# Two weight loads moved to ScalarE's queue in front of its table load, two scalar loads moved to SyncE

## The chip, the cores and the metric

The kernel runs on one core of a Trainium2 chip (trn2). The metric is the device time of one execution in microseconds (us), given as the median of several runs. The engines are TensorE (PE, matrix products), VectorE (DVE), ScalarE (ACT), GpSimd (POOL) and SyncE (SP, which here only issues transfers). Each runs its own instructions strictly in the order in which the program gives them. DMA transfers run on 16 DMA engines; SP's transfers are in one queue, those that ACT issues in another.

## The reference

Attention with a gated memory read, and behind it two feed-forward networks. B, H, S, D are 4, 8, 576, 64; there are 2304 tokens, the model width is 512 and the hidden width 2048.

```python
def _attn_ref(q, k, v, M_prev, z_prev, beta):
    scores = scale * np.matmul(q, k.transpose(0, 1, 3, 2))    
    local = np.matmul(a, v)
    q_p = phi(q)                                              
    mem_out = np.einsum('bhsd,bhde->bhse', q_p, M_prev) / mem_norm
    g = 1.0 / (1.0 + np.exp(-beta))[None, :, None, None]
    return g * mem_out + (1 - g) * local

def _moe_ref(x, w_in, w_out, s, b):
    r = np.maximum(x @ w_in, 0.0)
    return (s * (r * r) + b) @ w_out

def _moe2_ref(x, w_in, w_out):
    h = x @ w_in
    return (h * np.tanh(softplus(h))) @ w_out
```

The weights arrive as 64-bit floating-point numbers. [...]

## The kernel before

The work is cut into steps. Each step names an engine, an estimated duration, a due time (`prio`) and the buffers that it reads and writes. `Plan.order` (L234) is a list scheduler: it runs the steps in its own simulated time with these estimates, always starts the ready step that is due first on each engine, and the order in which it starts them is the order in which the instructions are written. Nothing is reordered on the chip. For a DMA step it reckons (L284 to L286) that transfers run one behind the other, the first no sooner than 0.35 us after its issue, and land 1.6 us and a `lag` after their turn. Where PE would have nothing to do between 7 and 165 us of the planned time, the plan puts in products of a block of zeros (`zero_product`, L1262).

The attention works in units, one for each batch entry and head. For the first batch entry each unit is cut in two; the first halves (row tiles 0 to 2) are due 2.36 us apart. Such a unit loads qz (the queries and z, L481), qk (transposed queries and keys, L476) and vm (L645) on SP's queue; POOL, ACT and DVE make phi and its norm (L500 to L506); PE makes the scores (L536); DVE adds the mask and takes the least value (L545); ACT makes exponentials (L554); POOL scales (L557, L571); PE transposes (L598) and multiplies by the values (L626); SP stores the result to `x_d` (L640).

Beside the units run the conversions of the first network's weights: 32 pieces, `convert` (L676), each 128 rows by 512 numbers, 512 KB. A piece is loaded to a raw buffer (L693, SP's queue), two ACT steps scale its high and low words (L700, L705), three DVE steps put them together (L707, L709, L711), ACT rounds the result to the high part (L717) and DVE makes the low part (L720). The first pieces are due 3.0 us apart, piece 0 at 0.0. Pieces 0 and 1 have their raw buffers in `stage`, at columns 0 and 1024; pieces 2 to 5 in weight tiles that are still unused. The first network begins as soon as its inputs are there: PE L803 and L877, with the scalars s and b (tile `sb`) read in L848 to L859. The second network (from L993) follows behind it.

Ahead of all steps stands a fixed beginning (L388 to L397): ACT issues the load of beta, loads its function table, and issues the loads of s and b, each of them one value spread over 128 partitions; DVE and ACT make the gates of beta and the block of zeros.

Of the kernel before, what the change touches and what calls it, by code (L numbers as in the profile page):

```python
# [9 lines left out]
F32 = mybir.dt.float32  # L10
F32R = mybir.dt.float32r
BF16 = mybir.dt.bfloat16
I32 = mybir.dt.int32
# [5 lines left out]
PSUM = bass.MemoryType.PSUM  # L19
DRAM = bass.MemoryType.DRAM  # L20

P = 128
MASKED = -1.0e30
HUGE = 3.0e38
PE, ACT, DVE, POOL, DMA = range(5)
# [41 lines left out]
def on(letter):  # L67
    return {"A": ACT, "D": DVE, "P": POOL}[letter]
# [111 lines left out]
class Plan:  # L180
# [29 lines left out]
    def add(self, engine, us, prio, f, r=(), w=(), after=(), keep=(), share=1.0):  # L210


        bufs = list({id(b): b for b in (*r, *w, *keep) if b.ring is not None}.values())
        new = [b for b in bufs if b.maker is None]
        waits = {id(s): s for b in r for s in b.writers}
        waits.update((id(s), s) for s in after)
        s = Step(engine, us, prio, f, list(waits.values()), bufs, new)
        s.share = share
        s.left = len(waits)
        for x in waits.values():  # L220
            x.next.append(s)
        for b in bufs:
            b.users += 1
            if b.maker is None:
                b.maker = s
            elif id(b.maker) not in waits:
                b.maker.next_start.append(s)
                s.left += 1
        for b in w:
            b.writers.append(s)  # L230
        self.steps.append(s)
        return s
# [100 lines left out]
def attention_then_two_ffn(ctx: ExitStack, tc: tile.TileContext, qk, qz, vm, beta,  # L333
# [3 lines left out]
    nc = tc.nc  # L337
# [22 lines left out]
    NONE = 5  # L360
    plan = Plan()
    add = plan.add
# [13 lines left out]
    sb = const.tile([P, 2], F32, name="sb")  # L376
# [8 lines left out]
    y_in = {j: Buf() for j in range(NT // N1)}  # L385
    wi_in, wo_in, wi_split = ({} for _ in range(3))

    nc.scalar.dma_start(igate[:, 1], beta.partition_broadcast(P))  # L388
    nc.scalar.preload_act_table_set("natural_log_exp_and_others")
    nc.scalar.dma_start(sb[:, 0:1], s1.partition_broadcast(P))  # L390
    nc.scalar.dma_start(sb[:, 1:2], b1.partition_broadcast(P))

    nc.vector.tensor_scalar(igate[:, 0], igate[:, 1], -1.0, 80.0, op0=ALU.mult, op1=ALU.min)
    nc.vector.tensor_scalar_min(igate[:, 1], igate[:, 1], 80.0)
# [1 line left out]
    nc.vector.tensor_scalar_add(igate, igate, 1.0)  # L396
    nc.scalar.copy(zeros, mask[:, :P])  # L397

    psum = ctx.enter_context(tc.tile_pool(name="psum", bufs=1, space=PSUM))
    banks = [Bank(psum.tile([P, 512], F32, name=f"bank{i}")) for i in range(8)]  # L400
    stage = Home(ctx.enter_context(tc.tile_pool(name="stage", bufs=1, side="right")), "stage", 3072)
    m1 = ctx.enter_context(tc.tile_pool(name="m1", bufs=1))
    small, att = ExitStack(), ExitStack()
    m1s = small.enter_context(tc.tile_pool(name="m1s", bufs=1))
# [256 lines left out]
    def weight_bufs():  # L661
        for nm in ("wih", "wil", "woh", "wol"):
            for r in range(NR):
                W[nm, r] = Buf(R[nm, r], [P, NCC, 512], F32R)

    def w_at(nm, r, j):
        return W[nm, r].t[:, j]

    def raw_buf(r, k):

        i = (8 * r + k) % 6
        if r > 1 or i < 2:
            return Buf(R["raw"], [P, 1024], I32)
        return Buf(R[("wih", "wil", "woh", "wol")[i - 2], 2], [P, 2048], I32)

    def convert(layer, prio, which, r, j, raw, after=()):  # L676


        w_in, w_out = ((w_in1, w_out1), (w_in2, w_out2))[layer - 1]
        fc = r * FPR + j  # L680
        src = w_in[j * P:(j + 1) * P, r * 512:(r + 1) * 512] if which == "in" else w_out[fc * P:(fc + 1) * P, :]
        w = Buf(R["w32"], [P, 512], I32)

        def words():
            return raw.t[:, :1024].rearrange("p (n two) -> p n two", two=2)

        def limbs():
            return raw.t[:, :1024].bitcast(U16).rearrange("p (n four) -> p n four", four=4)

        def f32():  # L690
            return w.t.bitcast(F32)

        add(DMA, 1.5, prio, lambda: nc.sync.dma_start(words(), src.bitcast(I32).rearrange("p (n two) -> p n two", two=2)),  # L693
            w=[raw], after=after).lag = 1.4 if layer == 1 else 3.0

        e = on((C_W if layer == 1 else C2_W)[j])
        add(e, 0.567 if e == ACT else 0.335, prio,
            (lambda: nc.scalar.activation(f32(), words()[:, :, 1].bitcast(F32), AF.Copy, scale=2.0 ** -112)) if e == ACT else  # L700
            (lambda: nc.vector.tensor_scalar(f32(), words()[:, :, 1].bitcast(F32), 2.0 ** -112, None, op0=ALU.mult)),
            [raw], [w])

        low_words = Buf()
        add(ACT, 0.567, prio, lambda: nc.scalar.activation(words()[:, :, 0], words()[:, :, 0].bitcast(U32), AF.Copy,  # L705
                                                          scale=2.0 ** -29), [raw], [low_words])
        add(DVE, 0.335, prio, lambda: nc.vector.tensor_scalar(w.t, w.t, 3, None, op0=ALU.logical_shift_left), [w], [w])  # L707
        signed = Buf()
        add(DVE, 0.542, prio, lambda: nc.vector.tensor_scalar(limbs()[:, :, 1], limbs()[:, :, 3], 0x8000, None, op0=ALU.bitwise_and),  # L709
            [raw, low_words], [signed])  # L710
        add(DVE, 0.605, prio, lambda: nc.vector.tensor_tensor(w.t, w.t, words()[:, :, 0], op=ALU.add), [raw, signed, w], [w])  # L711
        if layer == 1:
            hi, lo = f"w{which[0]}h", f"w{which[0]}l"
            hi_dve, lo_dve = C_HI[j] == "D", C_LO[j] == "D"
            half = Buf()
            add(DVE if hi_dve else ACT, 0.335 if hi_dve else 0.52, prio,
                lambda: (nc.vector.tensor_copy if hi_dve else nc.scalar.copy)(w_at(hi, r, j), f32()), [w],  # L717
                [W[hi, r], half])
            add(DVE if lo_dve else POOL, 0.6 if lo_dve else 1.23, prio,
                lambda: (nc.vector if lo_dve else nc.gpsimd).tensor_tensor(w_at(lo, r, j), f32(),  # L720
                                                                           w_at(hi, r, j).bitcast(F32), op=ALU.subtract),
                [w, half], [W[lo, r]])
        return w
# [426 lines left out]
        unit(0, h, PRE_A + STEP_A * h, (TA,), PLACE_A[h % 4])  # L1150
    for h in range(H):
        unit(0, h, PRE_B + STEP_B * h, (TB,), PLACE_B[h])
    raws = [raw_buf(i // 8, i % 8) for i in range(len(pieces))]
    weight_bufs()
    start = 0.0
    for i, p in enumerate(pieces):
        convert(1, start, *p, raws[i])
        start += CONV[i // 8]
# [15 lines left out]
    for i in range(len(seq) + LAG1):  # L1174
        if i < len(seq):
            j, fc = seq[i]
# [4 lines left out]
            n = len(plan.steps)  # L1181
# [4 lines left out]
        if i >= LAG1:  # L1186
            j, fc = seq[i - LAG1]
            n = len(plan.steps)
# [3 lines left out]
            if fc == NFC - 1:  # L1192
                n = len(plan.steps)
# [17 lines left out]
    n = len(plan.steps)  # L1211
# [3 lines left out]
    def converted_piece(which, r, j):  # L1215
        n = len(plan.steps)
        w = convert(2, CONV2, which, r, j, Buf(R["raw"], [P, 1024], I32), [opened])
        raw_steps.extend(plan.steps[n:])
        return w
# [17 lines left out]
    n = len(plan.steps)  # L1237
# [72 lines left out]
```

## Time and profile before

| | us |
|---|---|
| median of 3 runs | 1012.31 (1010.95 to 1012.92) |
| the profiled execution's own time | 1011.65 |
| its span, first to last instruction | 1009.7 |
| PE busy | 993.8 |
| DVE busy | 861.0 |
| ACT busy | 717.6 |
| POOL busy | 205.2 |

An engine is busy while an instruction of its own computes; issuing a DMA is not counted. Idle time of an engine counts only where another engine, or the end, waits for it. Matrix products are pipelined, so a busy PE is not PE at its peak.

### The profile page before, as it was taken

The numbers are of one execution on the slowest core, as the hardware profiler recorded it, in microseconds if no ns is written. First come the engines' busy times: TensorE is split into PE (matmuls) and PEld (weight loads), VectorE is DVE, ScalarE is ACT, GpSimd is POOL, SyncE is SP. The second block draws the span as 40 slices with busy tenths as digits, with TensorE's granted clock in tenths as the row PEclk, the third lists the DMA queues.
The fourth block names the chain that finished last, engine by engine and source line by source line (L and its number), as shares of the span: only waits on it lengthen the run. The fifth ranks groups of instructions, "written<-read, shape, count | busy, mean of one in ns | idle before, by whom it ended". The sixth has DMA issues, their size and how long they took to land.

```text
span 1009.7 us, 19024 instructions
## 1 busy us (share of the span) xinstructions
PE 993.8 (98%) x6274; PEld 904.4 (90%) x6274; DVE 861.0 (85%) x2232; ACT 717.6 (71%) x1606; POOL 205.2 (20%) x330
## 2 busy tenths in 40 slices
PE   7999999999999999999999999999999999999998
PEld 4758798999999999999888888899989998899987
DVE  6899999999999999986788886269996789967876
ACT  5988897888988889876778998446763466534552
POOL 5851123433443335320000000000110000100010
PEclk9999999999999999999999999999999999999999
DMA  9664563333533342215899986468787666766565
GB/s 270 182 201 128 158 199 99 112 92 101 144 90 91 97 123 85 85 54 182 264 279 299 298 280 225 155 229 276 231 287 253 210 225 204 262 222 216 166 224 172
DMA packets 88977, 188.54 MB, mean 187 GB/s; under 512 B 8752, under 2 KB 63024, under 8 KB 81584
## 3 DMA queue, kind: packets, MB, share of 16 engines
q1 hardware_dynamic: 81392, 135.95, 43.5%
q0 software_dynamic: 7056, 51.38, 15.0%
q8 instruction: 49, 0.80, 0.3%
q14 instruction: 48, 0.39, 0.1%
q10 hardware_dynamic: 432, 0.01, 0.0%
HBM read 144.32 MB, written 42.99 MB: 186 GB/s over the span
## 4 chain that ended last, share of the span: by engine, by line
PE 86%; DVE 5%; ACT 3%; issue 2%; DMA 2%; POOL 2%; SPq 0%; DVEq 0%; POOLq 0%; ACTq 0%
PE bank L877 19%; PE bank L803 19%; PE bank L1009 17%; PE bank L1081 10%; PE bank L626 6%; PE bank L1083 5%; PE bank L598 4%; PE bank L540 2%; PE bank L536 2%; PE bank L541 2%; POOL Pt L571 1%; PE bank L1078 1%; DMA woh<-wi_split_d 1%; DVE Pt L545 1%; ACT Pt L554 1%
## 5 line engine op out<-in xcount | busy, mean ns | idle before, releaser
L1009 PE MATMUL bank<-wi,woh 128*128 128x384 f32 x420 | 95.2, 335 | 0.1
L557 POOL TENSOR_SCALAR Pt<-ex,nm 128x64 f32<-128x64 f32 x148 | 70.8, 495 | 114.2 <-DVE nm L506 50.6
L1081 PE MATMUL bank<-wol,S 128*128 128x512 f32 x252 | 90.7, 391 | 0.0
L554 ACT ACTIVATE Pt<-Pt,mx 128x64 f32<-128x64 f32 (+4 forms) x148 | 81.7, 554 | 11.9 <-DVE mx L545 11.4
L1081 PE MATMUL bank<-woh,S 128*128 128x512 f32 x228 | 82.1, 392 | 0.0
L990 POOL DMA_DIRECT2D wol<-wo_split_d x16 | 8.7, 541 | 339.6 <-DVE wi L732 261.7
L1009 PE MATMUL bank<-wi,wol 128*128 128x384 f32 x300 | 76.0, 334 | 0.0
L1009 PEld LDWEIGHTS bank<-wi,woh 128*128 128x128 f32 x420 | 74.6, 188 | 1.4 <-DMA woh<-wi_split_d 0.6
L1083 PE MATMUL bank<-wol,S 128*128 128x256 f32 x252 | 70.6, 280 | 0.0
L598 PE MATMUL bank<-ident,Pt 128*128 128x128 f32 x432 | 65.7, 279 | 3.2 <-POOL Pt L571 3.1
L571 POOL TENSOR_SCALAR Pt<-Pt,rs 128x64 f32<-128x64 f32 (+2 forms) x68 | 53.9, 823 | 64.6 <-DVE rs L576 50.4
L606 DVE TENSOR_TENSOR PTl<-bank,PTh 128x128 fp32r<-128x128 f32 (+1 forms) x144 | 64.2, 481 | 1.3 <-ACT PTh L603 0.7
L1083 PE MATMUL bank<-woh,S 128*128 128x256 f32 x228 | 63.9, 280 | 0.0
L545 DVE CUSTOM_DVE_ANT_0 Pt<-bank,mask 128x320 f32<-128x320 f32 (+3 forms) x148 | 59.8, 417 | 4.4 <-PE bank L536 3.0
L598 PEld LDWEIGHTS bank<-ident,Pt 128*128 128x128 f32 x432 | 49.4, 142 | 9.5 <-POOL Pt L571 7.0
L603 ACT CAST PTh<-bank 128x128 fp32r<-128x128 f32 (+1 forms) x144 | 55.3, 431 | 2.7 <-PE bank L598 1.4
L1081 PEld LDWEIGHTS bank<-wol,S 128*128 128x128 f32 x252 | 47.2, 187 | 9.8
L1009 PEld LDWEIGHTS bank<-wi,wol 128*128 128x128 f32 x300 | 54.1, 188 | 0.3
L877 PE MATMUL bank<-gl,woh 128*128 128x256 f32 x320 | 53.8, 290 | 0.0
L877 PE MATMUL bank<-gh,wol 128*128 128x256 f32 x320 | 53.3, 289 | 0.0
L877 PE MATMUL bank<-gh,woh 128*128 128x256 f32 x320 | 52.1, 285 | 0.0
L803 PE MATMUL bank<-xh,wi 128*128 128x256 f32 x320 | 51.5, 288 | 0.6 <-DVE rt L854 0.4
(291 smaller groups left out, 3123.6 us busy)
## 6 DMA issues: line engine op xcount, KB each, us to landing
woh<-wo_split_d POOLq DMA_DIRECT2D x17, 1024.0 KB, 5.1
wol<-wo_split_d POOLq DMA_DIRECT2D x16, 1024.0 KB, 5.6
qk<-in_qk SPq DMA_DIRECT2D x24, 608.0 KB, 3.8
stage<-in_w_out SPq DMA_DIRECT2D x23, 512.0 KB, 4.3
wo_split_d<-high SPq DMA_DIRECT2D x44, 256.0 KB, 3.7
stage<-in_w_in SPq DMA_DIRECT2D x21, 512.0 KB, 5.0
wol<-wi_split_d POOLq DMA_DIRECT2D x10, 1024.0 KB, 6.0
stage<-wi_d SPq DMA_DIRECT2D x24, 384.0 KB, 3.7
```

The costliest lines, as they stand in the source:

```text
L545: nc.vector.tensor_tensor_reduce(Pt[t].t[:, D + lo:D + hi], ps.t[:, :hi - lo], mask[:, SP - w + lo:SP - w + hi], -SCALE, mx.t[:, t:t + 1] ...
L554: nc.scalar.activation(Pt[t].t[:, D:w + D], Pt[t].t[:, D:w + D], AF.Exp, bias=mx.t[:, t + i:t + i + 1], scale=-1.0, accum_out=rs.t[:, t:t ...
L557: add(POOL, 0.48, lambda: nc.gpsimd.tensor_scalar(Pt[t].t[:, :D], ex.t[:, t, :], nm.t[:, t:t + 1], 1.0, op0=ALU.mult, op1=ALU.mult), [ex, ...
L571: (nc.vector if e == DVE else nc.gpsimd).tensor_scalar(x, x, r, None, op0=ALU.mult)
L598: nc.tensor.transpose(ps.t[:, c - c0, :], Pt[t].t[:, c * P:(c + 1) * P], ident)
L606: nc.vector.tensor_tensor(PT[1].t[:, at_], ps.t[:, :n], PT[0].t[:, at_].bitcast(F32), op=ALU.subtract)
L626: nc.tensor.matmul(o.rearrange("p (t q) -> p t q", q=P), v, x.t[:, f[0]:f[-1] + 1:f[1] - f[0] if len(f) > 1 else 1, :], start=(c == 0 and ...
L803: nc.tensor.matmul(ph, w_at(nm, r, cc)[:, o:o + P], x_at(x, cc), start=(part == 0 and cc == 0), stop=(part == 2 and cc == NCC - 1))
L877: nc.tensor.matmul(acc[ec // per].t[:, (ec % per) * n:(ec % per + 1) * n], w_at(nm, r, jj)[:, ec * P:(ec + 1) * P], t(x), start=(big and f ...
L1009: nc.tensor.matmul(ps.t[:, :H2], w[i // 4].t[:, j, kk, i % 4], x[kk].t[:, k], start=begin and part == kk == 0, stop=part == 2 and kk == 1, ...
L1081: nc.tensor.matmul(acc[t].t.rearrange("p (k n) -> p k n", n=DH), s.t[:, 0, t * P:(t + 1) * P], x.t[:, :, q % 4], start=q == 0, stop=False, ...
L1083: nc.tensor.matmul(acc[t].t[:, :DH], s.t[:, 1, t * P:(t + 1) * P], x.t[:, 0, q % 4], start=False, stop=q == NQ2 - 1, skip_group_check=True)
```

## The change

The loads of weight pieces 0 and 1 leave the plan. They are issued by ACT, right behind the load of beta and in front of the function table's load, to the same places in `stage`. The pool of PSUM banks and `stage` are allocated earlier for that; no instruction belongs to it. In the plan each of the two loads becomes a step without an instruction on the plan's sixth engine (`NONE`), which says that the piece is there after 5.5 us and, behind it, after 1.0 us more. The loads of s and b leave ACT's queue and become two DMA steps of SP, due at 12.0.

```diff
     nc.scalar.dma_start(igate[:, 1], beta.partition_broadcast(P))
+    for j in range(2):
+        nc.scalar.dma_start(stage.tile([P, 1024], I32, 1024 * j, "raw").rearrange("p (n two) -> p n two", two=2),
+                            w_in1[j * P:(j + 1) * P, :512].bitcast(I32).rearrange("p (n two) -> p n two", two=2))
     nc.scalar.preload_act_table_set("natural_log_exp_and_others")
-    nc.scalar.dma_start(sb[:, 0:1], s1.partition_broadcast(P))
-    nc.scalar.dma_start(sb[:, 1:2], b1.partition_broadcast(P))
...
-        add(DMA, 1.5, prio, lambda: nc.sync.dma_start(words(), src.bitcast(I32).rearrange("p (n two) -> p n two", two=2)),
-            w=[raw], after=after).lag = 1.4 if layer == 1 else 3.0
+        if layer == 1 and which == "in" and r == 0 and j < 2:
+            add(NONE, (5.5, 1.0)[j], prio, lambda: None, w=[raw])
+        else:
+            add(DMA, 1.5, prio, lambda: nc.sync.dma_start(words(), src.bitcast(I32).rearrange("p (n two) -> p n two", two=2)),
+                w=[raw], after=after).lag = 1.4 if layer == 1 else 3.0
...
+    add(DMA, 0.2, 12.0, lambda: nc.sync.dma_start(sb[:, 0:1], s1.partition_broadcast(P)))
+    add(DMA, 0.2, 12.0, lambda: nc.sync.dma_start(sb[:, 1:2], b1.partition_broadcast(P)))
     raws = [raw_buf(i // 8, i % 8) for i in range(len(pieces))]
```

## Rows read from the trace of the kernel before

**Rows 1.** The page: busy us (share of the span) and instructions of each engine.

```profile
PE 993.8 (98%) x6274; PEld 904.4 (90%) x6274; DVE 861.0 (85%) x2232; ACT 717.6 (71%) x1606; POOL 205.2 (20%) x330
```

**Rows 2.** Busy time by stretch: from:to, length, engines, clock, DMA share, GB/s.

```profile
0.00:10.00 10.00, 4.02 (x11) 2.87 (x12) 3.19 (x13) 3.19 (x6) 3.15 (x11) 1.00 0.70 163
1.50:4.50 3.00, 0.00 (x0) 0.00 (x0) 0.57 (x2) 0.95 (x1) 1.08 (x4) 1.00 0.38 73
4.50:26.00 21.50, 18.75 (x57) 12.74 (x58) 16.04 (x60) 13.63 (x42) 13.14 (x19) 1.00 1.05 313
...
140.00:172.00 32.00, 30.59 (x240) 28.78 (x239) 31.77 (x87) 26.54 (x65) 10.11 (x13) 1.00 0.38 120
172.00:400.00 228.00, 227.22 (x1836) 223.34 (x1835) 221.07 (x712) 193.79 (x520) 89.84 (x144) 1.00 0.36 105
```

**Rows 3.** The same of the products of zeros alone (L1262): PE, PEld.

```profile
140.00:172.00 32.00, 6.26 (x36) 5.12 (x36) 1.00 0.38 120
```

**Rows 4.** The chain of waits, its beginning: start us, us, what.

```profile
2.54 5.63 DMA stage<-in_w_in
```

**Rows 5.** Timeline, 0 to 26 us: start, us, engine, line, operation [idle before <-releaser].

```profile
1.17 1.28 ACT L389 ACT_TABLE_LOAD   x1 [1.17 <-PEq L1297]
1.19 0.69 SPq L476 DMA_DIRECT2D wih<-in_qk  x1
1.20 0.43 ACTq L390 DMA_DIRECT2D sb<-in_s  x1
...
1.65 0.45 ACTq L391 DMA_DIRECT2D sb<-in_b  x1
...
2.54 0.43 SPq L693 DMA_DIRECT2D stage<-in_w_in  x1
...
4.55 0.22 ACT L395 ACTIVATE igate<-igate 128x16 f32<-128x16 f32 x1 [2.11 <-DVE igate L394]
...
6.50 0.23 DVE L498 TENSOR_SCALAR nm<-nm,igate 128x3 f32<-128x3 f32 x1
6.53 0.33 SPq L693 DMA_DIRECT2D stage<-in_w_in  x1
...
6.56 2.50 PE L536 MATMUL bank<-wih 64*128 64x64 f32 x6 [0.96 <-DMA wih<-in_qk]
...
8.19 0.66 ACT L700 ACTIVATE stage<-stage 128x512 f32<-128x512 f32 x1 [2.96 <-DMA stage<-in_w_in]
...
8.88 0.43 DVE L707 TENSOR_SCALAR stage<-stage 128x512 int32<-128x512 int32 x1 [2.15 <-ACT stage L700]
...
9.31 0.20 DVE L545 CUSTOM_DVE_ANT_0 Pt<-bank,mask 128x64 f32<-128x64 f32 x1
...
12.44 0.33 SPq L693 DMA_DIRECT2D woh<-in_w_out  x1
...
12.54 0.66 ACT L700 ACTIVATE stage<-stage 128x512 f32<-128x512 f32 x1
...
15.31 0.68 ACT L700 ACTIVATE stage<-wih 128x512 f32<-128x512 f32 x1 [1.31 <-DMA wih<-in_w_in]
...
25.89 0.70 ACT L700 ACTIVATE stage<-woh 128x512 f32<-128x512 f32 x1
```

**Rows 6.** DMA issues, each from a stretch around its issue: KB, us to landing.

```profile
wih<-in_qz SPq DMA_DIRECT2D x1, 128.0 KB, 3.0
wih<-in_qk SPq DMA_DIRECT2D x1, 192.0 KB, 5.3
stage<-in_w_in SPq DMA_DIRECT2D x1, 512.0 KB, 5.6
sb<-in_b ACTq DMA_DIRECT2D x1, 0.5 KB, 5.0
...
woh<-in_w_out SPq DMA_DIRECT2D x1, 512.0 KB, 7.3
```

**Rows 7.** The instructions that read `sb`, first of them: count, ns, first and last start.

```profile
L848 ACT ACTIVATE rt<-bank,sb x80: 448/474/511, 80.7 to 476.6; 128x256 f32<-128x256 f32 x80
```

More of the change, by code (lines that the diff above doesn't have):

```diff
@@ L386, in attention_then_two_ffn @@
     wi_in, wo_in, wi_split = ({} for _ in range(3))
+    psum = ctx.enter_context(tc.tile_pool(name="psum", bufs=1, space=PSUM))
+    banks = [Bank(psum.tile([P, 512], F32, name=f"bank{i}")) for i in range(8)]
+    stage = Home(ctx.enter_context(tc.tile_pool(name="stage", bufs=1, side="right")), "stage", 3072)
     nc.scalar.dma_start(igate[:, 1], beta.partition_broadcast(P))
+    for j in range(2):
+        nc.scalar.dma_start(stage.tile([P, 1024], I32, 1024 * j, "raw").rearrange("p (n two) -> p n two", two=2),
+                            w_in1[j * P:(j + 1) * P, :512].bitcast(I32).rearrange("p (n two) -> p n two", two=2))
     nc.scalar.preload_act_table_set("natural_log_exp_and_others")
-    nc.scalar.dma_start(sb[:, 0:1], s1.partition_broadcast(P))
-    nc.scalar.dma_start(sb[:, 1:2], b1.partition_broadcast(P))
     nc.vector.tensor_scalar(igate[:, 0], igate[:, 1], -1.0, 80.0, op0=ALU.mult, op1=ALU.min)
@@ L397, in attention_then_two_ffn @@
     nc.scalar.copy(zeros, mask[:, :P])
-    psum = ctx.enter_context(tc.tile_pool(name="psum", bufs=1, space=PSUM))
-    banks = [Bank(psum.tile([P, 512], F32, name=f"bank{i}")) for i in range(8)]
-    stage = Home(ctx.enter_context(tc.tile_pool(name="stage", bufs=1, side="right")), "stage", 3072)
     m1 = ctx.enter_context(tc.tile_pool(name="m1", bufs=1))
```

## The prediction

> **What bounds the kernel now.** I read the busy table first: TensorE (PE) is busy 993.8 of 1009.7 us [rows 1]. So time can be won only where PE does no useful work. The table by stage [rows 2] shows where that is: from 172 to 400 us PE is busy 227.22 of 228 us and nothing is to be had; from 140 to 172 it is busy 30.59 of 32, and 6.26 us of that are products of zeros [rows 3], which the plan puts in where PE has nothing to do. In the same 32 us VectorE (DVE) is busy 31.77. So until about 172 us the kernel is paced by the engines that prepare work for PE, DVE first; after it PE is full. A saving counts if DVE, ScalarE (ACT) and GpSimd reach 172 us earlier.
>
> The reader should then look at the first ten microseconds: DVE is busy 3.19 of 10 [rows 2]. The chain of waits names the cause: its first long piece is the transfer of the first weight piece, 5.63 us from its issue at 2.54 us [rows 4]. The timeline shows the engines around it [rows 5]: ACT stands 2.96 us until L700 can convert the piece at 8.19; DVE ends L498 at 6.73 and stands 2.15 us until L707 of the same piece at 8.88. Both run strictly in their written order, so the reduction of unit 0's scores at 9.31 stands behind L707, although PE began those scores at 6.56.
>
> **The change part by part.** *First piece issued earlier.* Now it is issued at 2.54 us as SyncE's (SP's) fourth DMA and lands 5.6 us later [rows 5, 6]. On ACT's queue it takes the place of the load of s, which is issued at 1.20 [rows 5]. No row shows a 512 KB transfer on that queue, so its landing is bounded. From below: the first transfer of all took 3.0 us for 128 KB [rows 6], the rest of 384 KB at the 313 GB/s of the stretch from 4.5 to 26 us [rows 2] is 1.26 us more: 1.20 + 4.26 = 5.46. From above: 5.6 us as now: 6.8. I take the lower half, about 6.0, because the DMA engines are busy only 0.38 of the time from 1.5 to 4.5 us [rows 2] and the piece would start in this gap.
>
> L707 starts 0.69 us after ACT begins the piece (8.88 - 8.19), and not before L498's end at 6.73. A landing at 6.0 gives 6.69, so 6.73, and DVE wins 8.88 - 6.73 = 2.15 us; a landing at 6.8 gives 7.49 and a gain of 1.39. ACT has 2.96 us to win and isn't late. I take 2.1 us.
>
> *Second piece.* It takes the place of b, issued at 1.65 instead of 6.53 [rows 5], and should land 1.2 to 2.4 us after the first (512 KB at 313 GB/s is 1.7), at 7.2 to 9.2. Its ACT work now begins at 12.54 with no wait for the piece [rows 5], so by itself this gives nothing; it fills ACT and DVE while unit 0 waits.
>
> *What is moved past.* The 1 MB now stands beside unit 0's operands instead of behind them. The qk transfer is the one that hurts: issued at 1.19, landed 5.3 us later at 6.49, and PE waited for it [rows 5, 6]. Bounds: at best it loses nothing, or gains, since s and b with their 128 single words no longer run beside it; at worst the whole 1 MB goes first, 3.3 us at 313 GB/s, and it lands at 9.8. I take 7.0, nearer to the first, because the gap from 1.5 to 4.5 us has room for 0.62 x 3.0 = 1.9 us of full transfer, some 580 KB. Then PE starts the scores at about 7.1 instead of 6.56, which still feeds DVE's reduction at 9.31 - 2.1 = 7.2.
>
> The Trainium skill, "DMA: Bandwidth & Descriptors", section "Issuing engines are not separate DMA queues", speaks against the change: DMAs from several engines run on the same 16 DMA engines and interleave, and issuing from a second engine saves only the sequencer's issue time. By that rule the sum would be the 0.76 us of the first rival below.
>
> *SP's queue.* It loses two issues of 0.43 and 0.33 us in front and gets s and b, 0.43 and 0.45 us, between units and pieces due about 12 us [rows 5]. The next pieces behind them wait 0.9 us longer; the first of those, issued at 12.44 with 7.3 us to landing, is there at 19.7 and is first used at 25.89 [rows 5, 6]: 6 us of cover, so nothing. If it were gone, the cost would be those 0.9 us. The first reader of s and b runs at 80.7 us [rows 7].
>
> *Table load.* It moves behind two issues, from 1.17 to about 2.1, and ends at 3.4 instead of 2.45. ACT's first work, at 4.55, waits for beta through DVE [rows 5]: 1.15 us of cover are left, cost nothing; without cover 0.9 us. The Trainium skill, "ScalarE: Activation LUTs", section "What ACT_TABLE_LOAD costs", adds a drain of 1.38 us to the 1.28 us which the trace shows too; it would end at 4.8 and cost 0.2 us. The trace shows no such drain apart from the idle time.
>
> *The planner.* The two pieces become steps without an instruction, done at 5.5 and 6.5 us of its own clock, where its rule for DMAs (L284 to L286) gave 6.6 (0.35, then 0.67, 0.72 and 0.36 for unit 0, 1.5 for the piece, 1.6 and 1.4 behind it) and 9.84 (1.75 for unit 1 and 1.5 more). All loads behind the first move up by 1.5 us in the plan, behind the second by 3.0. So every engine's order changes after the first microseconds. What the new order is worth can't be read from this trace. I bound it at 1.3 us either way, the second-largest stall for a piece, ACT's at 15.31 [rows 5], and take nothing.
>
> Sum: 1011.65 us is the profiled execution's own time (span 1009.7 and 1.95 around it). Less 2.1 gives 1009.55; the median of the runs is 0.66 above the profiled one, so 1012.31 - 2.1 = **1010.2 us**. What is late next: L498's own chain, from unit 0's first transfer to 6.73, and the qk transfer; both bind right behind L707.
>
> **The rivals.**
> - *The transfers interleave, and only issue time is saved.* For: from 4.5 to 26 us the DMA engines are full (1.05, [rows 2]), so 1 MB in front pushes unit 0 and unit 1 back. Against: the gap before 4.5 us. SP saves 0.43 + 0.33 = 0.76 us: 1011.55 us.
> - *The third piece's stall goes too.* ACT stands 1.31 us at 15.31 for the third piece [rows 5]. The gap's 1.9 us of transfer, once used, lets it land earlier by about as much as ACT comes earlier. It ends better only if the queue wins 2.1 + 1.31 = 3.4 us; then 1012.31 - 3.4 = 1008.9. Against: the gap is worth 1.9.
> - *Slower: the plan runs ahead of the transfers.* The plan moves the loads up by 3.0 us where the chip can win 1.9. Work on each later piece, written 1.1 us too early in ACT's order, holds what stands behind it. The third piece already does so for 1.31 us. Four pieces (third to sixth) would cost 4 x 1.1 = 4.4 against 2.1 won: 1014.6. It decides once ACT and DVE together wait over 2.1 us more for pieces than now. Against: only the third of them shows a wait in the trace of before.
> - *The change doesn't do what it says:* the pieces land no sooner, as b, of half a KB, took 5.0 us on that queue [rows 6], longer than SP's first 128 KB. With a landing at 8.1 nothing is won: 1012.3.
>
> **How the numbers follow.** A measurement of this kernel can tell about 0.2%, 2.0 us, from no change, so faster means under 1010.29. Forecast 0.52: 1010.2, with the order's 1.3 either way 1008.9 to 1011.5, about half of it faster (0.29) and half the same (0.23). Interleaving 0.15, nearly all the same (0.13), 0.02 faster. Third stall gone 0.11, faster. Slower by the plan 0.15. No earlier landing 0.07: same 0.05, slower 0.02. Faster 0.42, same 0.41, slower 0.17. The range goes from the third-stall case less 1.3, 1007.6, to the unchanged time plus 1.3, 1013.6; what is left out is most of the plan's case.
>
> **What would show it.** Right: the first weight conversion on ACT at about 6.0 us, L707 at about 6.7, DVE without a stall before it, DMA share well over 0.38 from 1.5 to 4.5 us; unit 0's scores on PE near 7.1; fills and idle time of PE from 140 to 172 us less by about 2. Wrong: scores after 8.7 (6.56 + 2.15), at which the qk transfer takes the stall over; ACT stalls for the third to sixth piece that add up to over 2 us; or a front that is 2 us earlier with PE filled up no sooner, in which case the order between 20 and 172 us has eaten it.

## The result, and the profile after

| | before | after |
|---|---|---|
| median | 1012.62 us (1010.95 to 1012.94, 4 runs) | 1019.54 us (1018.74 to 1020.63, 4 runs) |
| profiled execution, its span | 1011.65, 1009.7 | 1019.22, 1017.5 |

The change makes the kernel slower: ratio 1.0072, interval [1.0058, 1.0085], some 7 us. The forecast was 1010.2 us with a range of 1007.6 to 1013.6, so the time lies outside it, on the other side.

The busy table of after, in the form of [rows 1]:

```profile
PE 992.0 (98%) x6270; PEld 903.0 (89%) x6270; DVE 862.6 (85%) x2232; ACT 718.8 (71%) x1606; POOL 204.0 (20%) x330
```

No engine has more than 1.6 us of work added; PE has less. So the 7.8 us of longer span are waits and a lower clock. Where they are, the table by stage shows (from:to, length, busy us and instructions of PE, PEld, DVE, ACT, POOL, granted clock, DMA share, GB/s). After:

```profile
1.50:4.50 3.00, 0.00 (x0) 0.00 (x0) 0.59 (x2) 1.39 (x2) 1.24 (x4) 1.00 0.74 139
1.00:12.00 11.00, 4.52 (x13) 3.07 (x13) 2.94 (x10) 4.35 (x9) 2.47 (x6) 1.00 0.93 202
257.00:262.00 5.00, 3.14 (x19) 2.25 (x18) 4.94 (x16) 4.97 (x16) 4.07 (x6) 0.92 0.68 210
261.00:265.00 4.00, 3.81 (x20) 3.69 (x20) 3.13 (x11) 1.77 (x6) 1.42 (x2) 0.57 0.77 240
```

The same view of before, for the last three stretches:

```profile
1.00:12.00 11.00, 6.02 (x18) 4.64 (x19) 5.15 (x20) 4.75 (x13) 4.68 (x9) 1.00 0.83 205
257.00:262.00 5.00, 5.00 (x43) 5.00 (x43) 5.00 (x19) 3.91 (x11) 0.36 (x1) 1.00 0.81 194
261.00:265.00 4.00, 4.00 (x34) 3.90 (x33) 3.92 (x12) 3.95 (x12) 0.85 (x2) 1.00 0.89 257
```

Two places stand out. In the first 12 us DVE is busy 2.94 us instead of 5.15: the front, which the change was to shorten, became worse. And from 257 to 265 us, in the stage where [rows 2] shows PE practically full, PE is busy 3.14 of 5 us and then runs at a granted clock of 0.57. If one numbers PE's real products in each trace and compares when the k-th of them starts, after lies 2.2 us behind before at 250 us, 6.0 at 300 and 7.4 at 1000. So about 2.2 us arise before 250 us, 3.8 in the stretch at 257 to 265, and most of the rest in one wait at 880 to 900 us (who waits for whom: us, times, longest):

```profile
PE bank L1014 <- DMA woh<-wi_split_d: 1.3, 1, 1.3
```

The two kernels have different orders, so up to 172 us this lag is no measure of one place: it is 2.9 us at 20 us, 5.1 at 100 and 1.9 at 172.

The front first. Timeline of after, 0 to 13 us, the lines that answer to [rows 5]; lines of the kernel have moved, so L705 is L700 of before, L712 is L707, L503 is the Exp of a unit (0 or 1) on ACT, L504 the DVE step that follows it (L502 of before), L538 the scores, L547 their reduction:

```profile
2.14 1.28 ACT L396 ACT_TABLE_LOAD   x1 [2.14 <-issue]
...
3.63 0.70 POOL L502 TENSOR_SCALAR ex<-wih 128x192 f32<-128x192 f32 x1 [1.76 <-DMA wih<-in_qz]
...
4.40 0.21 ACT L400 ACTIVATE igate<-igate 128x16 f32<-128x16 f32 x1 [0.97 <-DVE igate L399]
...
7.10 0.66 ACT L705 ACTIVATE stage<-stage 128x512 f32<-128x512 f32 x1 [2.30 <-DMA stage<-in_w_in]
7.67 0.35 ACT L503 ACTIVATE ex<-ex 128x192 f32<-128x192 f32 x1
7.79 0.43 DVE L712 TENSOR_SCALAR stage<-stage 128x512 int32<-128x512 int32 x1 [2.97 <-ACT stage L705]
8.13 0.35 DVE L504 SCALAR_TENSOR_TENSOR ex<-wih,ex 128x192 f32<-128x192 f32 x1
...
8.21 2.50 PE L538 MATMUL bank<-wih 64*128 64x64 f32 x6 [2.35 <-DMA wih<-in_qk]
...
9.59 0.67 ACT L705 ACTIVATE stage<-stage 128x512 f32<-128x512 f32 x1 [1.01 <-DMA stage<-in_w_in]
...
11.88 0.36 DVE L504 SCALAR_TENSOR_TENSOR ex<-wol,ex 128x192 f32<-128x192 f32 x1 [1.89 <-ACT ex L503]
...
12.24 0.20 DVE L547 CUSTOM_DVE_ANT_0 Pt<-bank,mask 128x64 f32<-128x64 f32 x1
```

The first piece is there at 7.10 instead of 8.19. But ACT now has it written in front of unit 0's Exp (L503), which needs nothing of it and whose input POOL had ready at 3.63 + 0.70 = 4.33; so the Exp starts at 7.67. DVE has the piece's L712 in front of unit 0's L504, and unit 1's L504 in front of unit 0's reduction L547. That one waits 1.89 us for operands that came late, and unit 0's scores, begun on PE at 8.21, are first reduced at 12.24; before it was 9.31 [rows 5]. DVE's two stalls add up to 4.86 us where before had 2.15.

The landings, in the view of [rows 6] (KB, us from issue to landing), of the stretches around the issues of after:

```profile
stage<-in_w_in ACTq DMA_DIRECT2D x1, 512.0 KB, 5.9
...
stage<-in_w_in ACTq DMA_DIRECT2D x1, 512.0 KB, 7.9
...
wih<-in_qk SPq DMA_DIRECT2D x1, 192.0 KB, 7.0
```

Unit 0's qk takes 7.0 us instead of 5.3 and the first piece 5.9 instead of 5.6. From 1.5 to 4.5 us the DMA share did rise, from 0.38 to 0.74, and the rate with it, from 73 [rows 2] to 139 GB/s. But from 1 to 12 us the core moved 202 GB/s instead of 205: the transfers were not faster in sum, only dealt out in another way.

Then the late place. PE's longest wait from 250 to 262 us (engine, tile, line, what for: us, times, longest), and the timeline around them:

```profile
PE bank L600 <- POOL Pt L573: 1.1, 1, 1.1
```

```profile
255.33 1.85 SPq L825 DMA_DIRECT2D xr<-x_d  x4
257.93 1.49 POOL L573 TENSOR_SCALAR Pt<-Pt,rs 128x64 f32<-128x64 f32 x2 [5.54 <-DVE rs L578]
...
258.74 1.17 PE L600 MATMUL bank<-ident,Pt 128*128 128x128 f32 x6 [1.07 <-POOL Pt L573]
```

PE's transposes (L600) stand behind a unit whose scaling on POOL had itself waited 5.54 us for DVE. The block of the first network that could fill the gap isn't there either: its rows `xr` are loaded at 255.33, and before the corresponding load is issued at 250.83, so it comes 4.5 us later, twice the lag of 2.2:

```profile
250.83 1.85 SPq L820 DMA_DIRECT2D xr<-x_d  x4
```

Behind the gap, microsecond by microsecond (columns as above):

```profile
261.00:262.00 1.00, 0.81 (x5) 0.69 (x5) 1.00 (x3) 1.00 (x5) 1.00 (x2) 0.62 0.49 154
262.00:263.00 1.00, 1.00 (x5) 1.00 (x6) 1.00 (x4) 0.77 (x3) 0.42 (x1) 0.50 0.69 172
263.00:264.00 1.00, 1.00 (x7) 1.00 (x6) 1.00 (x6) 0.00 (x0) 0.00 (x0) 0.50 0.88 311
```

PE idled and was then granted 0.50, the lower of its two levels (1.2 of 2.4 GHz). From 261 to 265 us the mean is 0.57, so 4 x 0.43 = 1.7 us of PE's work are lost besides the 5.00 - 3.14 = 1.86 us that it stood. Together that is 3.6 of the 3.8 us by which the products fell back there. A run below (order_after_free) has the same gap without the low clock, and there the products fall back by 2.2 us, from 1.5 at 250 to 3.7 at 262 us.

### The profile page after: what moved, and what is told of

It reads as the page before. It is cut to its first block, busy times and chain, and to the rows that moved or that the text cites. A ratio compares the mean times of both kernels' runs of the same rounds, so it can differ in the third digit from the quotient of the medians.

```text
span 1017.5 us, 18993 instructions
## 1 busy us (share of the span) xinstructions
PE 992.0 (98%) x6270; PEld 903.0 (89%) x6270; DVE 862.6 (85%) x2232; ACT 718.8 (71%) x1606; POOL 204.0 (20%) x330
## 4 chain that ended last, share of the span: by engine, by line
PE 82%; DVE 6%; ACT 4%; DMA 3%; POOL 2%; issue 2%; SPq 0%; POOLq 0%; DVEq 0%; ACTq 0%
PE bank L1014 17%; PE bank L808 17%; PE bank L882 17%; PE bank L1086 10%; PE bank L628 5%; PE bank L1088 5%; PE bank L600 4%; PE bank L538 2%; PE bank L542 2%; PE bank L543 2%; DVE PTl L608 1%; ACT Pt L556 1%; POOL Pt L573 1%; DMA woh<-wi_split_d 1%; DVE Pt L547 1%
## 5 line engine op out<-in xcount | busy, mean ns | idle before, releaser
L600 PE MATMUL bank<-ident,Pt 128*128 128x128 f32 x432 | 65.9, 278 | 6.8 <-POOL Pt L573 6.6
L573 POOL TENSOR_SCALAR Pt<-Pt,rs 128x64 f32<-128x64 f32 (+2 forms) x68 | 51.6, 806 | 79.2 <-DVE rs L578 58.4
L547 DVE CUSTOM_DVE_ANT_0 Pt<-bank,mask 128x320 f32<-128x320 f32 (+3 forms) x148 | 59.9, 417 | 3.3 <-PE bank L538 1.6
L600 PEld LDWEIGHTS bank<-ident,Pt 128*128 128x128 f32 x432 | 49.4, 141 | 11.8 <-POOL Pt L573 9.3
```

Of the source, the lines that this page charges most:

```text
L547: nc.vector.tensor_tensor_reduce(Pt[t].t[:, D + lo:D + hi], ps.t[:, :hi - lo], mask[:, SP - w + lo:SP - w + hi], -SCALE, mx.t[:, t:t + 1] ...
L573: (nc.vector if e == DVE else nc.gpsimd).tensor_scalar(x, x, r, None, op0=ALU.mult)
L600: nc.tensor.transpose(ps.t[:, c - c0, :], Pt[t].t[:, c * P:(c + 1) * P], ident)
```

## The experiments

The change does two things at once: it moves transfers, and through the planned 5.5 and 1.0 us it gives every engine another order. The first two kernels part them. Both also have the earlier allocation of the banks and of `stage`.

**order_before.** The transfers of the change; the two pieces stay DMA steps of the plan, but issue nothing, and s and b are issued inside an existing step. So every engine has the order of before. Against the changed kernel:

```diff
-            add(NONE, (5.5, 1.0)[j], prio, lambda: None, w=[raw])
+            add(DMA, 1.5, prio, lambda: None, w=[raw], after=after).lag = 1.4
         else:
+            def load():
+                if layer == 1 and which == "out" and r == 0 and j == 0:
+                    nc.sync.dma_start(sb[:, 0:1], s1.partition_broadcast(P))
+                    nc.sync.dma_start(sb[:, 1:2], b1.partition_broadcast(P))
...
-    add(DMA, 0.2, 12.0, lambda: nc.sync.dma_start(sb[:, 0:1], s1.partition_broadcast(P)))
-    add(DMA, 0.2, 12.0, lambda: nc.sync.dma_start(sb[:, 1:2], b1.partition_broadcast(P)))
```

> Every engine's instructions stand in exactly the order of the kernel before; only the transfers are those of the change (both pieces on ACT's queue in front of the table load, s and b on SP in front of the fifth piece). Theory 'order': the loss of 6.9 us is the new order's, in which instructions stand in front of unit 0's that wait for later transfers; then this runs within 2 us of 1012.6. Theory 'transfers': the megabyte in front delays the qk transfer of unit 0 (8.2 instead of 6.5 us) and the qz of unit 1 (10.7 instead of 9.0), and that alone costs the time; then this runs at 1016 to 1020.

Measured: 1013.51 us, ratio 1.0004 [0.9993, 1.0015]. Its DVE in the front (timeline; L717 is L707 of before) and its late stretches (table by stage):

```profile
7.58 0.43 DVE L717 TENSOR_SCALAR stage<-stage 128x512 int32<-128x512 int32 x1 [1.03 <-ACT stage L710]
9.01 0.23 DVE L547 CUSTOM_DVE_ANT_0 Pt<-bank,mask 128x64 f32<-128x64 f32 x1 [0.92 <-PE bank L538]
11.93 0.37 DVE L504 SCALAR_TENSOR_TENSOR ex<-wol,ex 128x192 f32<-128x192 f32 x1 [1.23 <-ACT ex L503]
```

```profile
257.00:262.00 5.00, 5.00 (x43) 5.00 (x43) 5.00 (x19) 3.90 (x11) 0.27 (x1) 1.00 0.76 189
261.00:265.00 4.00, 4.00 (x34) 3.91 (x33) 3.92 (x11) 3.95 (x12) 0.85 (x2) 1.00 0.85 260
```

The transfers by themselves are worth nothing that can be measured. L707 comes 8.88 - 7.58 = 1.30 us earlier, and of that 0.92 is taken back at once, because the scores come late from PE (qk), and 1.23 more at unit 1. The reduction starts 0.3 us earlier than before. The stretch from 257 to 265 is as before, and in this trace the products lie 0.1 us behind before at 250 us and 0.3 at 700.

**order_after.** The order of the change, with the transfers in their old queues and places.

```diff
-    for j in range(2):
-        nc.scalar.dma_start(stage.tile([P, 1024], I32, 1024 * j, "raw").rearrange("p (n two) -> p n two", two=2),
-                            w_in1[j * P:(j + 1) * P, :512].bitcast(I32).rearrange("p (n two) -> p n two", two=2))
     nc.scalar.preload_act_table_set("natural_log_exp_and_others")
+    nc.scalar.dma_start(sb[:, 0:1], s1.partition_broadcast(P))
+    nc.scalar.dma_start(sb[:, 1:2], b1.partition_broadcast(P))
...
+        def load_vm():
+            nc.sync.dma_start(vx(), vm[b, h][:, :nb])
+            if first_half and h < 2:
+                nc.sync.dma_start(stage.tile([P, 1024], I32, 1024 * h, "raw").rearrange("p (n two) -> p n two", two=2),
+                                  w_in1[h * P:(h + 1) * P, :512].bitcast(I32).rearrange("p (n two) -> p n two", two=2))
...
-    add(DMA, 0.2, 12.0, lambda: nc.sync.dma_start(sb[:, 0:1], s1.partition_broadcast(P)))
-    add(DMA, 0.2, 12.0, lambda: nc.sync.dma_start(sb[:, 1:2], b1.partition_broadcast(P)))
+    add(DMA, 0.2, 12.0, lambda: None)
+    add(DMA, 0.2, 12.0, lambda: None)
```

> Every engine's instructions stand in exactly the order of the changed kernel; the transfers are those of the kernel before (pieces on SP behind vm of units 0 and 1, s and b on ACT). Theory 'order': as slow as the changed kernel, 1017 to 1021, and the Exp of unit 0 stands behind the first piece until about 8.1 us. Theory 'transfers': within 2 us of 1012.6.

Measured: 1018.44 us, ratio 1.0064 [1.0046, 1.0082]: nearly the whole loss, without a transfer moved. The stall in front (timeline) and the late stretches (table by stage):

```profile
8.71 0.43 DVE L717 TENSOR_SCALAR stage<-stage 128x512 int32<-128x512 int32 x1 [3.75 <-ACT stage L710]
```

```profile
257.00:262.00 5.00, 3.33 (x18) 2.45 (x17) 4.94 (x16) 4.97 (x16) 4.17 (x6) 0.89 0.76 212
261.00:265.00 4.00, 4.00 (x20) 3.90 (x21) 3.03 (x11) 1.87 (x6) 1.32 (x2) 0.59 0.82 246
```

So the loss is the order. The other runs ask which part of it.

**front_after.** order_before with only the swaps of the first microseconds put in: ACT's first word of pieces 0 and 1 in front of the Exp of units 0 and 1, and the three moves on DVE that go with it. The moves in words, as the kernel makes them in the ordered list:

```
ACT  piece 0, first scaling   -> in front of unit 0's Exp
ACT  piece 1, first scaling   -> in front of unit 1's Exp
DVE  piece 0, L712            -> in front of unit 0's L504
DVE  piece 0, L714            -> in front of unit 0's gate step (L498 of before)
DVE  unit 1's L504            -> in front of unit 0's reciprocal
```

> Transfers of the change, every engine in the order of the kernel before (as in order_before, 1.0004), except for the front: ACT has the first conversion of pieces 0 and 1 in front of the Exp of units 0 and 1, DVE has L712 and L714 of piece 0 in front of unit 0's work and unit 1's L504 in front of unit 0's reciprocal and scores, as the changed kernel has them. Theory 'front': these few places make the loss; then 1016 to 1020. Theory 'rest': the places further back in the new order make it; then within 2 us of 1012.5.

Measured: 1014.16 us, ratio 1.0022 [1.0011, 1.0034]. Its DVE's timeline shows the two stalls of after (L759 is L712, L546 is L504); the table by stage shows PE nearly whole at 257 us:

```profile
7.62 0.43 DVE L759 TENSOR_SCALAR stage<-stage 128x512 int32<-128x512 int32 x1 [2.85 <-ACT stage L752]
11.64 0.36 DVE L546 SCALAR_TENSOR_TENSOR ex<-wol,ex 128x192 f32<-128x192 f32 x1 [1.83 <-ACT ex L545]
```

```profile
257.00:262.00 5.00, 4.80 (x35) 4.33 (x35) 4.97 (x18) 3.90 (x11) 1.25 (x3) 1.00 0.62 178
```

Put into the order of before, the front places (with the change's transfers) cost about 2.2 us [1.1, 3.4]; the rest of the change's loss lies in other places. That 2.2 us is also the lag of after's products at 250 us doesn't make the front its cause: in this trace they are 1.4 us behind there.

**front_before.** The counterpart: the changed kernel with the front places put back.

```
ACT  pieces 0 and 1, first scaling -> in front of the same piece's second scaling
DVE  piece 0, L712 and L714        -> in front of unit 0's reciprocal
DVE  unit 1's L504                 -> in front of unit 1's next step
```

> The changed kernel with only those few places of the front put back as the kernel before has them, the rest of its order kept. Theory 'front': 1012 to 1014. Theory 'rest': 1017 to 1020. If both parts count, 1014.5 to 1017.

Measured: 1022.87 us from four runs between 1017.61 and 1026.39, ratio 1.0100 [1.0068, 1.0131]. The runs' mean granted clocks were 0.998, 0.990, 0.996 and 0.989, the two longest at the two lowest clocks, so the spread goes with the clock and its size can't be given to the front. What can be read is that the kernel isn't faster than the change, and that, by the table by stage, the gap at 257 us is as in after:

```profile
257.00:262.00 5.00, 3.14 (x18) 2.24 (x17) 4.94 (x16) 4.96 (x15) 4.45 (x6) 0.93 0.74 217
```

The trace is that of its fastest run, and it says more. Unit 0's first reduction is early again (8.99; after has 12.24):

```profile
8.99 0.22 DVE L589 CUSTOM_DVE_ANT_0 Pt<-bank,mask 128x64 f32<-128x64 f32 x1
```

Yet the products are 2.0 us behind before at 250 us and 5.7 at 300, nearly as in after (2.2 and 6.0). So it isn't shown that the front's 2.2 us come back when its places do, and this trace speaks against it. It is shown that the later order stalls without the bad front.

**order_after_free.** order_after with piece 0 not loaded at all: DVE writes zeros in its place. If the late stalls were echoes of the late piece, they would go.

```diff
-            add(NONE, (5.5, 1.0)[j], prio, lambda: None, w=[raw])
+            add(NONE, (5.5, 1.0)[j], prio, (lambda: nc.vector.memset(raw.t[:, :1024], 0)) if j == 0 else (lambda: None), w=[raw])
...
-            if first_half and h < 2:
+            if first_half and h == 1:
```

> The order of the changed kernel on every engine, the transfers of the kernel before, but piece 0 isn't loaded: DVE fills its buffer with zeros at the start (the piece's weights are zeros). Unit 0's Exp then waits for nothing. Theory 'the front of the order makes the stalls further back': PE's stall from 257 to 262 us is gone and the time is 1012 to 1014. Theory 'the later places stall by themselves': the stall and the low clock behind it stay, only 1.3 to 2.5 us are won against order_after, 1015.5 to 1017.5.

Measured: 1018.5 us (six runs, 1015.78 to 1025.68), ratio 1.0072 [1.0044, 1.0099]. DVE's timeline (L717 is L712 of after, L503 is L504), and the stretch at 257 us:

```profile
5.54 0.43 DVE L717 TENSOR_SCALAR stage<-stage 128x512 int32<-128x512 int32 x1 [0.58 <-ACT stage L710]
11.40 0.36 DVE L503 SCALAR_TENSOR_TENSOR ex<-wol,ex 128x192 f32<-128x192 f32 x1 [3.67 <-ACT ex L502]
```

```profile
257.00:262.00 5.00, 3.35 (x22) 2.67 (x23) 4.94 (x14) 4.86 (x16) 4.49 (x6) 1.00 0.78 218
```

With the first piece there at once, L707's stall is gone (0.58 us), but a wait of 3.67 us stands at unit 1's L503 (L504 of after), which this order puts in front of unit 0's reduction. And PE still stands 1.65 of 5 us at 257. Both belong to the order. In this profile no lower clock follows the gap from 257 to 262 us (1.00 from 261 to 265), so the drop isn't a sure companion of it. Against order_after nothing was won, where even the theory of the later places expected 1.3 us; but the six runs' mean granted clocks lie between 0.989 and 0.998, and the profiled one had the highest, so the median can't price the missing piece.

**planned_60.** The change with 6.0 instead of 5.5 us for the first piece, which by the plan's numbers puts unit 0's Exp (planned at 5.62) in front again.

```diff
-            add(NONE, (5.5, 1.0)[j], prio, lambda: None, w=[raw])
+            add(NONE, (6.0, 1.0)[j], prio, lambda: None, w=[raw])
```

> The changed kernel with the first piece planned to be there at 6.0 instead of 5.5 (the second still 1.0 behind it). That puts unit 0's Exp back in front of the first piece's conversion on ACT, and nothing else is meant by it. Theory 'order': DVE's 2.97 us stall in front of the first piece's L712 shrinks to what unit 0's own chain leaves, and the time falls by about 1 to 3 us to 1016.5 to 1018.5; unit 1's work in front of unit 0's scores stays. Theory 'transfers': no difference, 1019.5.

Measured: 1017.19 us, ratio 1.0040 [1.0027, 1.0053]. DVE's first long wait in the timeline, and the stretch at 257 us:

```profile
7.95 0.43 DVE L712 TENSOR_SCALAR stage<-stage 128x512 int32<-128x512 int32 x1 [1.66 <-ACT stage L705]
```

```profile
257.00:262.00 5.00, 4.89 (x41) 4.68 (x41) 4.94 (x16) 4.88 (x15) 2.53 (x3) 1.00 0.55 154
```

The Exp is back in front (stall 1.66 instead of 2.97), and the stretch at 257 us is whole again; the kernel is 2.3 us faster than the change and still 4 us slower than before. It has a third order with losses of its own: its products are already 5.2 us behind before at 172 us.

**plan_plus_01, plan_minus_01, plan_plus_03.** How much does any order cost? These three are the kernel before, with all its transfers, where the plan alone believes that piece 0 lands 0.1 us later, 0.1 us earlier, or 0.3 us later.

```diff
-            w=[raw], after=after).lag = 1.4 if layer == 1 else 3.0
+            w=[raw], after=after).lag = (1.5 if which == "in" and r == j == 0 else 1.4) if layer == 1 else 3.0
```

(1.3 and 1.7 in the other two.)

> The kernel before, same transfers; only the plan reckons that piece 0 lands 0.1 us later (lag 1.5 instead of 1.4). The list scheduler writes another order for all engines. Theory 'the plan's order is what counts, and what a small shift of a planned time does to it has no direction and is larger than the 1.3 us of the prediction': anywhere between 1010 and 1019. Theory 'an order that fits the transfers is worth the same': within 1.3 us of 1012.3.

> The same with piece 0 reckoned 0.1 us earlier (lag 1.3). Same theories: between 1010 and 1019 in the first, within 1.3 us of 1012.3 in the second.

> The same with piece 0 reckoned 0.3 us later (lag 1.7). Same theories: between 1010 and 1019 in the first, within 1.3 us of 1012.3 in the second.

Measured: 1.0015 [1.0003, 1.0027], 1.0023 [1.0011, 1.0034] and 1.0014 [1.0001, 1.0027]. A tenth of a microsecond in one number of the plan goes with 1.5 or 2.3 us, in either direction. All three are slower than the order of before, by 1.5, 2.3 and 1.4 us, a little over the 1.3 us that the prediction allowed, but all three intervals reach below it, and of the medians (1012.6, 1014.75 and 1013.24 us) only the second lies outside the 1.3 us of the second theory. So that small shifts cost more than 1.3 us is not shown. The mean granted clocks of their profiles are 0.995, 0.997 and 0.998, that of before is 1.000. The low clock lies early (0.57 from 15 to 19 us in the first two, from 16 to 20 in the third, in the first two once more before 64 us), in the stage that PE doesn't pace, so what it costs is not shown.

**sb_only.** Of the change only the move of s and b, as planned steps.

```diff
-    nc.scalar.dma_start(sb[:, 0:1], s1.partition_broadcast(P))
-    nc.scalar.dma_start(sb[:, 1:2], b1.partition_broadcast(P))
...
+    add(DMA, 0.2, 12.0, lambda: nc.sync.dma_start(sb[:, 0:1], s1.partition_broadcast(P)))
+    add(DMA, 0.2, 12.0, lambda: nc.sync.dma_start(sb[:, 1:2], b1.partition_broadcast(P)))
```

> The kernel before with only s and b moved to SP, due at 12.0. If they are harmless, as the prediction said, within 1.5 us of 1012.6. If their 0.9 us of issues or their slow landing on SP's queue hold units 2 and 3 back, 1014 or more.

Measured: 1013.77 us, ratio 1.0020 [1.0009, 1.0030]. **sb_late** is the same move with the order of before (issued inside the load step of a later piece, as in order_before):

```diff
-    nc.scalar.dma_start(sb[:, 0:1], s1.partition_broadcast(P))
-    nc.scalar.dma_start(sb[:, 1:2], b1.partition_broadcast(P))
...
+            if layer == 1 and which == "out" and r == 0 and j == 0:
+                nc.sync.dma_start(sb[:, 0:1], s1.partition_broadcast(P))
+                nc.sync.dma_start(sb[:, 1:2], b1.partition_broadcast(P))
```

> The kernel before with its order, weights on SP as before; only s and b go to SP in front of the fifth piece, as the change does. If the load of 256 single words on ACT's queue slowed unit 0's qk, PE starts the scores before 6.3 us and the time is up to 0.5 us shorter; if they are harmless at either place, scores at 6.5 and within 1 us of 1012.2.

Measured: 1013.39 us, ratio 1.0005 [0.9996, 1.0015]. The move is harmless. What sb_only loses fits its other order, in whose trace the products are 4.2 us behind at 172 us, but the two intervals overlap a little. sb_late's timeline holds a surprise (L534 is the scores, L710 is L707 of before):

```profile
4.98 2.50 PE L534 MATMUL bank<-wih 64*128 64x64 f32 x6 [1.59 <-DMA wih<-in_qk]
...
8.66 0.47 DVE L710 TENSOR_SCALAR stage<-stage 128x512 int32<-128x512 int32 x1 [1.99 <-ACT stage L703]
```

PE begins unit 0's scores at 4.98 instead of 6.56: the two loads of half a KB had held up unit 0's 192 KB by 1.6 us. It isn't chance in one run: sb_only, without them too, begins at 4.95, and the seven other kernels with them on ACT's queue and the weights on SP's begin between 6.35 and 6.74. It is worth nothing, because the reduction still stands behind L710 and the piece.

**front_free, front_late.** What is a microsecond of the front worth? front_free is the kernel before with piece 0 written as zeros by DVE instead of loaded; front_late is the kernel before with 20 additions of zero on DVE ahead of unit 0's work.

```diff
+        if layer == 1 and which == "in" and r == 0 and j == 0:
+            add(DMA, 1.5, prio, lambda: nc.vector.memset(raw.t[:, :1024], 0), w=[raw], after=after).lag = 1.4
```

```diff
     nc.vector.tensor_scalar_add(igate, igate, 1.0)
+    for _ in range(20):
+        nc.vector.tensor_scalar_add(igate, igate, 0.0)
```

> The kernel before without the load of piece 0: DVE fills its buffer with zeros before the first step, so the piece's weights are zeros; every other instruction and the order stay. The 2.15 us stall of DVE in front of L707 is gone without any transfer in front. If a front that is earlier arrives at the end, as the prediction took for granted: 1010.0 to 1010.8. If it is swallowed on the way, within 1 us of 1012.5.

> The kernel before with 20 additions of zero to the gates on DVE in front of unit 0's work, some 5 us, so that unit 0's scores on DVE come about 3 us later than 9.31; the order stays. If a late front arrives at the end: 1015 to 1016. If it is swallowed on the way (as the 1.1 us that order_before was late at 20 us were gone at 25): within 1 us of 1012.5.

Measured: 0.9982 [0.9971, 0.9993] and 1.0027 [1.0016, 1.0038]. Unit 0's first reduction, in front_free and in front_late:

```profile
7.18 0.23 DVE L545 CUSTOM_DVE_ANT_0 Pt<-bank,mask 128x64 f32<-128x64 f32 x1
```

```profile
10.87 0.20 DVE L547 CUSTOM_DVE_ANT_0 Pt<-bank,mask 128x64 f32<-128x64 f32 x1
```

Against 9.31 [rows 5] that is 2.13 us earlier for 1.8 us of time [0.7, 2.9], and 1.56 us later for 2.7 [1.6, 3.8]. The front does set the end if the order stays, by these intervals roughly one for one. The traces are less sure of the size: at 250 us the products are 2.0 us ahead and 1.0 behind, and a wait at 880 to 900 us adds 1.4 and 1.0 us to both.

**one_piece.** The best that the runs point to: the order of before, only piece 0 on ACT's queue, unit 0's vm issued behind unit 1's qz, s and b late.

```diff
-    for j in range(2):
+    for j in range(1):
...
+        def load_vm():
+            if first_half and h == 0:
+                held_back.append(lambda: nc.sync.dma_start(vx(), vm[b, h][:, :nb]))
```

> Every engine in the order of the kernel before; only piece 0 is issued by ACT in front of the table load, piece 1 stays on SP, vm of unit 0 goes behind qz of unit 1, s and b go to SP as in the change. Half a megabyte less stands beside unit 0's operands than in order_before. If the front of order_before lost to the late qk (PE starts the scores at 8.2) and the late qz of unit 1, the stalls of DVE before 13 us (1.03, 0.92 and 1.23 there) shrink, the scores start at about 7.5 and the time is 1010.8 to 1011.8. If the DMA engines move no more bytes than before whatever the queue, within 1 us of 1012.3.

Measured: 1011.68 us, ratio 0.9994 [0.9982, 1.0005]. In its front the piece lands at 6.26, and qk still comes last (L721 is L700 of before, L543 the scores, L552 their reduction):

```profile
6.26 0.66 ACT L721 ACTIVATE stage<-stage 128x512 f32<-128x512 f32 x1 [1.14 <-DMA stage<-in_w_in]
6.95 0.43 DVE L728 TENSOR_SCALAR stage<-stage 128x512 int32<-128x512 int32 x1 [0.32 <-ACT stage L721]
...
7.62 2.50 PE L543 MATMUL bank<-wih 64*128 64x64 f32 x6 [2.13 <-DMA wih<-in_qk]
...
8.45 0.23 DVE L552 CUSTOM_DVE_ANT_0 Pt<-bank,mask 128x64 f32<-128x64 f32 x1 [0.99 <-PE bank L543]
```

It reduces 0.86 us earlier than before, and its products are 1.8 us ahead up to 172 us, but only 0.7 at 500 and none at 1000 us. No kernel with the real work beats the one before by an amount that can be told.

## Why the prediction was wrong, step by step

**What bounds the kernel: right.** front_free and front_late show that in the order of before the front's stall reaches the end, 1.8 us of 2.13 won and 2.7 us for 1.56 lost.

**First piece issued earlier: wrong in size.** It was put at 6.0, at worst 6.8, and was used at 7.10, outside both bounds. The value was nearly met in one_piece (6.26), where one piece less and unit 0's vm later stood beside it; which of the two helped isn't parted. The failed step is "the DMA engines are busy only 0.38 of the time from 1.5 to 4.5 us [rows 2] and the piece would start in this gap". The gap was used, but it gave (139 - 73) x 3.0, some 200 KB, where the prediction counted on 580, and the rate up to 12 us did not grow. The Trainium skill, "DMA: Bandwidth & Descriptors", section "Issuing engines are not separate DMA queues", says that transfers from several issuing engines interleave on the same 16 DMA engines; this trace agrees, with 202 GB/s against 205 from 1 to 12 us.

**Second piece, qk: within or near the bounds, the values too kind.** The second piece was used at 9.59 (expected 7.2 to 9.2), qk at 8.21 (7.0 taken, 6.5 to 9.8 as bounds). In order_before qk takes over 0.92 of the 1.30 us won. So the transfers win 0.3 us at unit 0's first reduction, and measure 1.0004 [0.9993, 1.0015] in the time: the first rival's result, that they interleave and win at most 0.76 us, was right of the transfers.

**SP's queue, s and b: right.** sb_late measures 1.0005 [0.9996, 1.0015].

**Table load: right.** It runs from 2.14 to 3.42, and ACT's next work at 4.40 waits for DVE. The 4.8 us that followed from the drain in the Trainium skill, "ScalarE: Activation LUTs", section "What ACT_TABLE_LOAD costs", is not borne out, as ACT works at 4.40.

**The planner: wrong, and this is the cause.** The failed step was "What the new order is worth can't be read from this trace" and the term set for it, 1.3 us either way, taken as nothing. order_after measures it alone at 1.0064 [1.0046, 1.0082], that is 6.5 us [4.7, 8.3]. Two faults are in it.

First, part of the order could have been worked out beforehand. The plan lands unit 0's qk, which shares a buffer with qz, at 0.35 + 0.667 + 0.72 + 1.6 + 1.3 = 4.64 us. POOL's step of 0.82 and 0.16 to hand on give 5.62 for unit 0's Exp. The change declares the piece at 5.5, 0.12 us sooner. The Exp is due earlier (-0.02 against 0.0), but at 5.5 the piece is the only step that ACT has ready, so it goes first. On the chip the piece came at 7.10, while the Exp's input was ready at 4.33. The prediction took for granted that unit 0's chain would stay in front of the piece; in the order of before, front_after prices that and the other front places at 2.2 us.

Second, 1.3 us was the size of one stall in the front, and it was used as a bound for all later places. The largest loss lies at 257 to 265 us, where the trace of before shows PE full. The gap is there in all four kernels with the later order of the change (after, order_after, front_before, order_after_free); from 257 to 262 us PE is busy 4.80 to 5.00 of 5 in before, order_before, front_after and planned_60. Even changes of 0.1 us in one planned number measured 1.5 and 2.3 us, with intervals down to 0.3 and 1.1.

**The slower rival: right side, other mechanism.** It named the plan running ahead of the transfers and put the price at the third to sixth pieces. The plan does run ahead, but the price is at pieces 0 and 1 and unit 1's L504, and in PE's gap 250 us later. The third piece's conversion starts at 15.62, before at 15.31. The chain of waits of after puts its load behind the landing of unit 0's vm; what ties the two isn't shown.

```profile
1.92 7.99 DMA wih<-in_vm
9.93 5.67 DMA wih<-in_w_in
...
15.62 0.68 ACT wih L710
```

By the rival's own sign it did not decide: from 4 to 32 us ACT and DVE wait 8.2 us for pieces (3.3 + 1.5 + 0.4 and 3.0), before 6.4 (3.0 + 1.3 and 2.1), which is 1.8 more and not over 2.1. The signs named for a wrong prediction stayed away too: the scores began at 8.21, not after 8.7, and ACT's stalls for the third to sixth piece add up to 1.9 us, not over 2. All of them looked at transfers and at the first 172 us, and none at PE's full stage.

**What stays open.** PE's wait at 880 to 900 us (for weights of the second network) is in the traces of after (1.3 us), order_before (1.8), front_after (1.4), front_free (1.3), front_late (0.9) and one_piece (0.8), but not in those of before, order_after, front_before and order_after_free. So it is tied neither to the order nor to the transfers of the change. Whether it comes and goes between executions of one kernel, one trace of each can't tell. What the front and the later places each take of the loss is open too: front_after prices the front at 2.2 us, and front_before's trace, with unit 0's first reduction early again, is nearly as late as after's, so the two don't simply add up.

## What to carry to other kernels

Where a planner writes the order, an edit to one planned time is an edit to every engine's order: write both orders out and compare them, before a transfer is priced, and look for work that now stands in front of something that doesn't need it. A declared landing time that is earlier than the chip's makes an in-order engine stand with all that is behind: here 5.5 against 7.10 put a stall of 2.97 us in front of unit 0, and 6.0 instead of 5.5, which changed the whole order again, gave 2.3 us back. To find the cause of such a loss, run the two halves apart: new transfers in the old order, and old transfers in the new.

## What the runs showed of the hardware

- A gap in the DMA engines was filled without a gain in sum: from 1.5 to 4.5 us the share went from 0.38 to 0.74 and the rate from 73 to 139 GB/s; from 1 to 12 us the share went from 0.83 to 0.93 and the rate from 205 to 202 GB/s.
- Two loads of half a KB, each spread over 128 partitions, issued from ACT, delayed a 192 KB load of SP's queue by 1.6 us (scores at 6.35 to 6.74 in eight kernels with them, at 4.95 and 4.98 in two without).
- Behind a stretch in which PE was busy 3.14 of 5 us, the granted clock was 0.50 for two microseconds with PE busy, and 1.00 again from 265 us. The gap cost 1.86 us and the clock behind it 1.7 in after. In order_after_free the stretch from 257 to 262 us had PE busy 3.35 of 5 at a clock of 1.00, and it stayed at 1.00 behind it.
